# Block 3's row statistics, scale and stores ahead of the first form of wr and wi; the second chunk's forms a unit later; block 1's third column turned second

## The chip, the cores and the metric

The kernel runs on one core of one Trainium2 chip. The metric is the device time of one execution, in microseconds. Before the change it is 850.71 us, the median of three runs (850.18 to 850.97).

## The reference, cut to what matters

```python
xn = layernorm(x)                      # x: 2048 x 640, float32
a = xn @ wr.T ; b = xn @ wi.T          # the DFT over the 640 columns, as two matrices
A = cr @ a - ci @ b                    # the DFT over the 2048 rows, real part alone
B = gelu(xn @ w1 + b1) @ w2 + b2       # w1: 640 x 1536, w2: 1536 x 640
out = x + A + B
```

cr and ci are 2048 x 2048 (`dft_seq_re`, `dft_seq_im`), wr and wi are 640 x 640 (`dft_hid_re`, `dft_hid_im`).

## The kernel before, in words

Every operand of a matmul is a pair: a part rounded to fp32r ("hi") and what is left of the float32 value ("lo"). A product is three matmuls: hi by hi, hi by lo, lo by hi (`product`, lines 278 to 280). `split` makes such a pair: an ACTIVATE on ScalarE writes hi (line 160), a TENSOR_TENSOR on VectorE subtracts it from the value and writes lo (line 161). So each pair that TensorE uses has passed ScalarE and then VectorE, and both work strictly in the order in which the program is written; nothing is reordered by a scheduler.

The 2048 rows are four blocks of 512 (block 0 to 3), each four chunks of 128 rows (c = 0 to 15). The MLP (B) is worked block by block; the first two blocks unit by unit, where a unit is one of the 12 pieces of 128 columns of w1. With g counting units over both blocks (g = 12 + i in block 1), unit i of block 1 issues on TensorE the 15 matmuls of `hidden(g + 2)` (line 304) and then the 15 of `output(g)` (lines 278 to 280). Between them lie `gelu(g + 2)`: on ScalarE the Gelu out of the bank (line 322) and the hi part (line 326), on VectorE the lo part (line 328); the result "hs" is what `output(g + 2)` reads two units later. Below, hs(17) means that pair for g = 17.

Beside those units run three side works, and their place in the program is what the change is about:

- the layer norm of the later blocks: `ln_stats` (BN_STATS and BN_AGGR on VectorE, lines 185 and 186), `ln_scale` (a Sqrt on ScalarE, line 192, which makes ScalarE load another table of functions, and five small VectorE steps), `ln_apply` (line 201), and stores of the rows to an HBM buffer `xs` (line 203). Chunks 12 and 13 are stored by the queue of GpSimd, 14 and 15 by that of SyncE. `load_z(t)` reads block t back from `xs` in another order (line 234), and `turn_z2`, `turn_z1` transpose it (lines 786 and 792);
- the forms of wr and wi, `prep_w(s)`: chunk j = s // 3 of the five chunks of columns, step k = s % 3. Step 0 transposes two tiles that `load_w` brought (line 396, loads at line 388); each step then splits two or three pieces into the staging tile `wst` and GpSimd's queue stores them to the HBM buffers `wit` (line 418). `wst` has room for one step's pieces, so the splits of a step wait until stores of the step before have landed. In order the stores of a chunk are w0, w1 (step 0), w6, w2 (step 1), w3, w4, w5 (step 2). Six steps, two chunks, lie in the units of block 1 (`w_early`); the others come later;
- the forms of blocks 2 and 3 for a version of the first MLP product with fewer multiplications (`form_of`, `sums_w1`, `split_w1`, with the tile `tw`).

After unit 10 the bank sums of block 1 are turned: `add_block` adds the bias on ScalarE (line 368), transposes the bank on VectorE (line 371) and adds it to the rows on GpSimd (line 373). Column e lies in bank 3 + e. `head`, `mid` and `finish` are the products of the version with fewer multiplications; `head(1)` writes first to bank 5, column 2, and then to bank 6, column 3.

SyncE's queue carries nearly all loads and the SyncE stores, in the program's order; GpSimd's carries the other stores and GpSimd's own adds.

Of the kernel before, what the change touches and what calls it, by code (L numbers as in the profile page):

```python
# [26 lines left out]
def kernel(  # L27
# [152 lines left out]
    def ln_stats(c):  # L180
        m = MV
        st = ST[c % 2]
        half = D // 2
        for h in range(2):
            nc.vector.bn_stats(st[:, h, :], xt[c][:, h * half : (h + 1) * half])
        nc.vector.bn_aggr(m[:, c % 4, 0:2], st.rearrange("p a b -> p (a b)"))
# [12 lines left out]
    def ln_apply(c, queue=nc.sync):  # L199
        m = MV[:, c % 4]  # L200
        nc.vector.tensor_scalar(xt[c], xt[c], m[:, 0:1], m[:, 3:4], op0=ALU.subtract, op1=ALU.mult)
        for k in range(NC):
            queue.dma_start(xs[c % NC * NC + k, c // NC * B : (c // NC + 1) * B], xt[c][k * B : (k + 1) * B])  # L203
# [20 lines left out]
    ZT = mr.tile([P, 2, TB], F32, name="zt")  # L224
# [4 lines left out]
    def load_z(t):  # L229
        z = out_pool.tile([P, NB, DQ], F32, tag="zo", bufs=1, name=f"z{t}")  # L230
        Z["z"] = z
        for q in range(Q):
            v = xs[:, t * B : (t + 1) * B, q * DQ : (q + 1) * DQ].rearrange("n r d -> r n d")
            nc.sync.dma_start(z[q * B : (q + 1) * B], v)
# [124 lines left out]
    def load_xo(t):  # L359

        xo[t] = out_pool.tile([P, NB, DQ], F32, tag="zo", bufs=1, name=f"xo{t}")
        for q in range(Q):
            nc.sync.dma_start(xo[t][q * B : (q + 1) * B], rows_of(x, t)[:, :, q * DQ : (q + 1) * DQ])
# [414 lines left out]
    def form_of(name, cc, src, dst):  # L778
        FX[name, cc] = dst
        split(dst[:, 0], dst[:, 1], src)  # L780

    def lane(tag, k):
        return whole[tag][:, k * 2 * TB : (k + 1) * 2 * TB].rearrange("p (a b) -> p a b", a=2)
# [21 lines left out]
    def sums_w1(q):  # L805
        if q >= NF // 2:
            return
        r = RQ[q]
        low = r[:, 0:2].rearrange("p c (g f) -> p g c f", g=2)
        high = r[:, :, P:].rearrange("p (k c) f -> p k c f", k=2)  # L810
        add(low, high, low, ALU.subtract)
        add(r[:, 2:4, P:], r[:, 2:4, P:], r[:, 0:2, :P], ALU.subtract)
        add(r[:, 2:4, :P], r[:, 2:4, :P], r[:, 2:4, P:], ALU.subtract)

    def split_w1(q):
        if q >= NF // 2:
            return
        TW[q] = A["tw"].tile([P, 2, 8 * P], F32R, tag=f"tw{q % 2}", bufs=1, name=f"tw{q}")
        split(TW[q][:, 0], TW[q][:, 1], RQ.pop(q).rearrange("p a b -> p (a b)"))
        TW[q] = TW[q].rearrange("p a (c f) -> p a c f", c=4)  # L820
# [149 lines left out]
    def open_tw():  # L970
        A["es"].close()
        A["w"] = None
        A["es"] = ExitStack()
        A["tw"] = pool("twp", stack=A["es"])
# [9 lines left out]
    def second_block(i):  # L984

        if i == 0:
            load_z(2)
            ln_stats(12)
            ln_stats(13)
        if i == 1:  # L990
            ln_stats(14)
            ln_stats(15)
        if i == 2:
            ln_scale(12, 4)
            for c in range(12, 16):
                ln_apply(c, nc.gpsimd if c < 14 else nc.sync)
        if i == 3:
            A["zs"] = place("xc01", (P, 30 * P), F32, name="zs")
            turn_z2(two(0), 0)
            turn_z2(two(2), 2)  # L1000
            turn_z1(ZT[:, 0], 4)
            load_z(3)
        if i == 4:
            form_of("a11", 0, two(0)[:, 0], lane("as", 5))
            open_xf()
        if i == 5:
            form_of("a11", 1, two(0)[:, 1], lane("xc23", 0))
            form_of("oa", 0, ZT[:, 0], lane("xc23", 1))
        if i == 6:
            form_of("a12", 0, two(2)[:, 0], lane("xc23", 2))  # L1010
            turn_z2(ZT, 2)
            turn_z2(two(4), 0)
            turn_z1(A["zs"][:, 6 * TB : 7 * TB], 4)
            load_xo(1)
            open_tw()
        if i == 7:
            sums_w1(0)
            split_w1(0)
            load_rq(1)
            form_of("a22", 0, ZT[:, 0], lane("r01", 0))  # L1020
        if i == 8:
            form_of("a22", 1, ZT[:, 1], lane("r01", 1))
            add(ZT, ZT, two(4))
        if i == 9:
            form_of("s1", 0, ZT[:, 0], lane("r01", 2))
            form_of("s1", 1, ZT[:, 1], lane("r01", 3))
            add(two(4), two(0), two(4), ALU.subtract)
            add(ZT, ZT, two(0), ALU.subtract)
# [18 lines left out]
        form_of("s4", 0, two(2)[:, 0], XTT[:, 3])  # L1047
        form_of("s4", 1, two(2)[:, 1], XTT[:, 4])

    w_early = {0: (0,), 1: (1,), 2: (2,), 3: (3,), 4: (4,), 5: (5,)}  # L1050
    prep_w1(3)
    gelu(1, acc1)
    for g in range(NG):
        t, i = divmod(g, NF)
        if t == 0:
            if i:
                prep_w1(i + 3)
            prep_w2(i + 1)
            load_w1(i + 6)
            load_w2(i + 4)  # L1060
            if i != 8:
                first_block(i)
            if i == NF - 1:
                open_w()
                acc = hidden(g + 2)
                output(g)

                def fill(k):
                    for e in ((0,), (1, 2))[k]:
                        add_block(xo[0], e, oacc[0][e], f"ot0_{e}", bias=b2c[:, e : e + 1])  # L1070

                gelu(g + 2, acc, fill)
                outs(0, (3, 4))
            elif i == NF - 2:
                output(g)
                gelu(g + 2, hidden(g + 2))
            else:
                acc = hidden(g + 2) if g else acc2
                if i == NF - 3:
                    for j in range(ND):  # L1080
                        prep_xt(1, j)
                        if j + 2 < ND:
                            transpose_z(1, j + 2)
                gelu(g + 2, acc)
                if i == 8:
                    first_block(i)
                if i == 9:
                    ln_stats(10)
                    ln_stats(11)
                output(g)  # L1090
        elif i < NF - 2:
            acc = hidden(g + 2)
            gelu(g + 2, acc)
            output(g)
            second_block(i)
            for k in w_early.get(i, ()):
                prep_w(k)
        elif i == NF - 2:
            output(g)
            forms_s2()  # L1100
            head(0)
            forms_s3()
        else:
            output(g)
# [36 lines left out]
        outs_at((3, 4), (0, 1), done=True)  # L1141

    outs(1, (0,), yt=lambda n: AB[:, 0], done=False)
    forms_ob()
    outs_at((2, 1), (4, 5))
    mid(0, rest)
    forms_s4()
    head(1)
# [106 lines left out]
    for n in range(1, 2 * NF):  # L1255
        blk, i = divmod(n, NF)
# [549 lines left out]
```

## Time and profile before

| | us |
|---|---|
| median of three runs | 850.71 (850.18 to 850.97) |
| the profiled execution's own time | 853.42 |
| its span on the core | 851.6 |
| TensorE busy in the span | 842.5 |
| VectorE busy | 668.0 |
| ScalarE busy | 355.3 |
| GpSimd busy | 53.6 |

Times in views of the profile are microseconds from the start of the span. PE is TensorE's matmuls, DVE is VectorE, ACT is ScalarE, POOL is GpSimd, SP is SyncE; a q behind a name means the engine's sequencer, which waits and issues. A timeline row has the start, the duration, the engine, the line, the operation with what it writes and reads, how many like ones follow each other, and in brackets for how long the engine was idle before it and what ended that. In the view of waits a row has the waiting instruction, what it waited for, the sum, the number and the longest. The granted clock of TensorE is 0.999 of full speed over the span.

### The profile page before, as it was taken

The page shows a single profiled execution, that of the slowest core. Times are in us where ns is not written, and L with a number is a line of the kernel's source. Part 1 is how long each engine was busy: PE and PEld are TensorE (multiplying, and loading weights), DVE is VectorE, ACT ScalarE, POOL GpSimd, SP SyncE. Part 2 cuts the span into 40 slices and gives each one's busy share as a digit, 9 for nine tenths or more (in the row PEclk, how much of TensorE's full clock was granted, in tenths as well). Part 3 has the DMA queues.
Part 4 walks back from the last instruction along what each step waited for, and adds up shares of the span by engine and source line. Part 5 has one row for each costly group of instructions (what it writes and reads, how often), then busy time and mean ns, then how long its engine had stood idle before and what let it go on. Part 6 is the DMA issues. An engine that isn't in the chain of part 4 may idle for free.

```text
span 851.6 us, 10345 instructions
## 1 busy us (share of the span) xinstructions
PE 842.5 (99%) x3707; PEld 694.5 (82%) x3707; DVE 668.0 (78%) x841; ACT 355.3 (42%) x499; POOL 53.6 (6%) x78
## 2 busy tenths in 40 slices
PE   8999999999999999999999999999999999999997
PEld 6888888778888888888888888888888888888886
DVE  6766764795757888879988787899977898885687
ACT  7454533555655554333434343232322423223241
POOL 0000313131221300000000000000000000000001
PEclk9999999999999999999999999999999999999999
DMA  6667799738669998948743669763865879805464
GB/s 185 187 185 186 162 215 252 196 79 195 207 216 347 360 218 158 188 102 204 164 137 95 177 211 285 171 139 97 213 164 171 253 184 228 312 18 179 124 170 108
DMA packets 207363, 158.45 MB, mean 186 GB/s; under 512 B 81040, under 2 KB 180880, under 8 KB 206800
## 3 DMA queue, kind: packets, MB, share of 16 engines
q1 hardware_dynamic: 198368, 134.59, 62.2%
q0 software_dynamic: 4400, 21.89, 6.5%
q10 hardware_dynamic: 4544, 1.31, 0.6%
q8 instruction: 29, 0.48, 0.2%
q14 instruction: 22, 0.18, 0.1%
HBM read 114.76 MB, written 42.99 MB: 185 GB/s over the span
## 4 chain that ended last, share of the span: by engine, by line
PE 83%; DVE 4%; DMA 4%; ACT 3%; issue 3%; SPq 2%; POOL 1%; ACTq 0%; POOLq 0%; DVEq 0%
PE banks L278 27%; PE banks L279 26%; PE banks L280 26%; PE banks L304 3%; DMA x<-in_A_x_dram 1%; DMA wit<-wst 1%; SPq L388 1%; DMA xs<-x 1%; ACT ab L322 1%; SPq L203 0%; SPq L178 0%; POOL wit L418 0%; DVE r L161 0%; ACT hs L326 0%; DVE tw L161 0%
## 5 line engine op out<-in xcount | busy, mean ns | idle before, releaser
L278 PE MATMUL banks<-as,xab 128*128 128x512 f32 x411 | 160.0, 389 | 0.6 <-DVE zs L371 0.6
L279 PE MATMUL banks<-as,xab 128*128 128x512 f32 x411 | 159.9, 389 | 0.0
L280 PE MATMUL banks<-as,xab 128*128 128x512 f32 x411 | 159.9, 389 | 0.0
L160 ACT ACTIVATE as<-r 128x1024 fp32r<-128x1024 f32 x80 | 85.0, 1062 | 177.9 <-PE banks L280 149.5
L161 DVE TENSOR_TENSOR as<-r,as 128x1024 fp32r<-128x1024 f32 x80 | 97.1, 1215 | 41.5 <-ACT as L160 41.5
L278 PEld LDWEIGHTS banks<-as,xab 128*128 128x128 f32 x411 | 77.2, 188 | 17.0 <-DVE zs L371 1.0
L279 PEld LDWEIGHTS banks<-as,xab 128*128 128x128 f32 x411 | 77.2, 188 | 16.0
L280 PEld LDWEIGHTS banks<-as,xab 128*128 128x128 f32 x411 | 77.2, 188 | 15.9
L278 PE MATMUL banks<-as,xc 128*128 128x512 f32 x224 | 87.1, 389 | 0.0
L279 PE MATMUL banks<-as,xc 128*128 128x512 f32 x224 | 87.1, 389 | 0.0
L280 PE MATMUL banks<-as,xc 128*128 128x512 f32 x224 | 87.1, 389 | 0.0
L160 ACT ACTIVATE as<-rt 128x1024 fp32r<-128x1024 f32 x32 | 34.0, 1063 | 70.5 <-PE banks L280 62.5
L304 PE MATMUL banks<-xtt,xab 128*128 128x512 f32 x240 | 57.2, 391 | 0.2 <-ACT xtt L160 0.2
L304 PEld LDWEIGHTS banks<-xtt,xab 128*128 128x128 f32 x240 | 44.7, 188 | 10.1 <-ACT xtt L160 0.6
L278 PEld LDWEIGHTS banks<-as,xc 128*128 128x128 f32 x224 | 42.1, 188 | 8.8
L280 PEld LDWEIGHTS banks<-as,xc 128*128 128x128 f32 x224 | 42.1, 188 | 8.7
L279 PEld LDWEIGHTS banks<-as,xc 128*128 128x128 f32 x224 | 42.0, 188 | 8.7
L161 DVE TENSOR_TENSOR as<-rt,as 128x1024 fp32r<-128x1024 f32 x32 | 38.8, 1211 | 5.3 <-ACT as L160 5.3
L160 ACT ACTIVATE as<-u 128x1024 fp32r<-128x1024 f32 (+1 forms) x24 | 22.1, 919 | 48.2 <-PE banks L280 48.2
L512 DVE STREAM_TRANSPOSE r<-raw 128x1024 f32<-128x1024 f32 x32 | 39.5, 1239 | 3.0 <-PE banks L280 2.4
L161 DVE TENSOR_TENSOR as<-u,as 128x1024 fp32r<-128x1024 f32 (+1 forms) x24 | 24.9, 1041 | 18.8 <-ACT as L160 18.8
L512 DVE STREAM_TRANSPOSE rt<-raw 128x1024 f32<-128x1024 f32 x32 | 38.8, 1229 | 0.9 <-PE banks L280 0.8
(353 smaller groups left out, 1622.9 us busy)
## 6 DMA issues: line engine op xcount, KB each, us to landing
raw<-in_A_dft_seq_re_dram SPq DMA_DIRECT2D x64, 256.0 KB, 5.5
raw<-in_A_dft_seq_im_dram SPq DMA_DIRECT2D x64, 256.0 KB, 5.1
ws<-wit SPq DMA_DIRECT2D x15, 384.0 KB, 5.8
xo<-in_A_x_dram SPq DMA_DIRECT2D x16, 320.0 KB, 5.9
xab<-wit SPq DMA_DIRECT2D x13, 384.0 KB, 4.0
wit<-wstp POOLq DMA_DIRECT2D x12, 384.0 KB, 3.7
x<-in_A_x_dram SPq DMA_DIRECT2D x14, 320.0 KB, 4.4
xs<-x SPq DMA_DIRECT2D x56, 80.0 KB, 1.8
```

The costliest lines, as they stand in the source:

```text
L160: nc.scalar.activation(h, s, AF.Copy)
L161: nc.vector.tensor_tensor(l, s, h.bitcast(F32), op=ALU.subtract)
L278: nc.tensor.matmul(acc, wh, mh, start=first, stop=False, skip_group_check=goes_on)
L279: nc.tensor.matmul(acc, wh, ml, start=False, stop=False, skip_group_check=goes_on)
L280: nc.tensor.matmul(acc, wl, mh, start=False, stop=last, skip_group_check=goes_on)
L304: nc.tensor.matmul(acc, W1[i][:, a, j * P : (j + 1) * P], XT[j][:, b], start=n == 0, stop=n == len(steps) - 1)
L322: nc.scalar.activation(a, acc, AF.Gelu_apprx_tanh, bias=b1c[:, i : i + 1])
L388: nc.sync.dma_start(t[q * B : (q + 1) * B], v[:, :, s0 : s0 + B])
L512: nc.vector.transpose(held(pieces[g][2], u).rearrange("p c (n i) -> p c n i", i=B), r.rearrange("p n (c i) -> p c n i", i=B))
```

## The change

Three things are written in another place; no operation is added or removed.

- All of the layer norm of block 3 (statistics of chunks 12 to 15, scale, apply, stores) stands in unit 0 ahead of `prep_w(0)`; before, it was spread over units 0 to 2. `load_z(2)` is issued behind the stores, not ahead of everything.
- The steps of the second chunk of wr and wi move one unit: `prep_w(3)` from unit 3 to unit 4, `prep_w(4)` from 4 to 5, `prep_w(5)` from 5 to 6. `split_w1(0)` and `load_rq(1)` move from unit 7 to unit 8, behind the Gelu of that unit.
- Of block 1's columns, column 2 is turned second, ahead of `forms_ob`; before, it was turned behind it. Column 1 stays behind it.

```diff
     def second_block(i):
         if i == 0:
-            load_z(2)
-            ln_stats(12)
-            ln_stats(13)
-        if i == 1:
-            ln_stats(14)
-            ln_stats(15)
-        if i == 2:
+            for c in range(12, 16):
+                ln_stats(c)
             ln_scale(12, 4)
             for c in range(12, 16):
                 ln_apply(c, nc.gpsimd if c < 14 else nc.sync)
+            load_z(2)
...
             load_xo(1)
+            prep_w(5)
             open_tw()
         if i == 7:
             sums_w1(0)
+            form_of("a22", 0, ZT[:, 0], lane("r01", 0))
+        if i == 8:
             split_w1(0)
             load_rq(1)
-            form_of("a22", 0, ZT[:, 0], lane("r01", 0))
-        if i == 8:
             form_of("a22", 1, ZT[:, 1], lane("r01", 1))
...
-    w_early = {0: (0,), 1: (1,), 2: (2,), 3: (3,), 4: (4,), 5: (5,)}
+    w_early = {0: 0, 1: 1, 2: 2, 4: 3, 5: 4}
...
     outs(1, (0,), yt=lambda n: AB[:, 0], done=False)
+    outs_at((2,), (4,))
     forms_ob()
-    outs_at((2, 1), (4, 5))
+    outs_at((1,), (5,))
     mid(0, rest)
```

What that does to the order on the engines is shown at three places. In all of them `wt`, `wraw` belong to wr and wi, `wst` is the staging tile of their forms, `x` are rows of block 3, `z` is a block read back.

SyncE's queue, behind the stores of block 0's result (`ys`, line 930): the stores of chunks 14 and 15 and the read of block 2 change places.

```order
 L930 DMA ys_62<-xo_842 2048x1x32
-L234 DMA z_1018<-xs 32x16x160 x4
-L388 DMA wraw_1_1033<-in_A_dft_hid_re_dram 32x20x32 x4
-L388 DMA wraw_1_1038<-in_A_dft_hid_im_dram 32x20x32 x4
 L203 DMA xs<-x_877 32x640 x4
 L203 DMA xs<-x_879 32x640 x4
+L234 DMA z_1056<-xs 32x16x160 x4
+L388 DMA wraw_1_1065<-in_A_dft_hid_re_dram 32x20x32 x4
+L388 DMA wraw_1_1070<-in_A_dft_hid_im_dram 32x20x32 x4
 L234 DMA z_1212<-xs 32x16x160 x4
```

The eight stores stood behind the second load of wr and wi and now stand ahead of the read of block 2.

GpSimd's queue, behind the adds of block 0's result:

```order
 L373 TENSOR_TENSOR xo_842<-xo_842,ot_4_979 128x16x32
+L203 DMA xs<-x_873 32x640 x4
+L203 DMA xs<-x_875 32x640 x4
 L418 DMA wit_63<-wst 128x768
 L418 DMA wit_64<-wst 128x768
 L418 DMA wit_69<-wst 128x768
 L418 DMA wit_65<-wst 128x768
-L203 DMA xs<-x_873 32x640 x4
-L203 DMA xs<-x_875 32x640 x4
 L418 DMA wit_66<-wst 128x512
```

The eight stores of chunks 12 and 13 stood behind the first four stores of forms and now stand ahead of them.

VectorE, from the end of unit 10 to the sums that `finish(0)` needs (`ab`, `zs` take the turned columns, `tw` and `hs` are `split_w1(1)` and the form "ob" of `forms_ob`):

```order
 L161 TENSOR_TENSOR xtt<-zs,xtt 128x512 x2
 L371 STREAM_TRANSPOSE ab<-banks 128x512
+L371 STREAM_TRANSPOSE zs<-banks 128x512
 L452 TENSOR_TENSOR zs<-zs,zt 128x1024
-L161 TENSOR_TENSOR tw_1567<-rq_1424,tw_1567 128x1024
+L161 TENSOR_TENSOR tw_1570<-rq_1459,tw_1570 128x1024
 L161 TENSOR_TENSOR hs<-zs,hs 128x512
-L371 STREAM_TRANSPOSE zs<-banks 128x512 x4
+L371 STREAM_TRANSPOSE zs<-banks 128x512 x3
 L452 TENSOR_TENSOR banks<-banks,fifth 128x512 x2
```

One transposition of 128x512 stands ahead of the three steps of `forms_ob` and not behind them.

More of the change, by code (lines that the diff above doesn't have):

```diff
@@ L1095 @@
             second_block(i)
-            for k in w_early.get(i, ()):
-                prep_w(k)
+            if i in w_early:
+                prep_w(w_early[i])
         elif i == NF - 2:
```

## The prediction

> **What bounds the kernel now.** I read the page first, then the waits of TensorE, then TensorE's timeline where it waits, and from there the timelines of the engines it waits for.
>
> ```profile
> span 851.6 us, 10345 instructions
> ...
> PE banks L279 <- DVE hs L328: 0.6, 1, 0.6
> PE banks L278 <- DVE zs L371: 0.6, 1, 0.6
> PE banks L278 <- ACT hs L326: 0.4, 1, 0.4
> ...
> 139.70 3.56 PE L304 MATMUL banks<-xtt,as 128*128 128x512 f32 x15
> ...
> 146.87 3.56 PE L304 MATMUL banks<-xtt,as 128*128 128x512 f32 x15
> 150.83 0.49 PE L278 MATMUL banks<-hs,r 128*128 128x512 f32 x1 [0.39 <-ACT hs L326]
> 151.91 0.50 PE L279 MATMUL banks<-hs,r 128*128 128x512 f32 x1 [0.58 <-DVE hs L328]
> ...
> 155.21 3.56 PE L304 MATMUL banks<-xtt,xab 128*128 128x512 f32 x15
> ...
> 162.01 3.56 PE L304 MATMUL banks<-xtt,xab 128*128 128x512 f32 x15
> ...
> 182.87 0.39 PE L280 MATMUL banks<-xtt,tw 128*128 128x512 f32 x1
> 183.83 0.50 PE L278 MATMUL banks<-as,xab 128*128 128x512 f32 x1 [0.58 <-DVE zs L371]
> ...
> 186.82 0.50 PE L278 MATMUL banks<-r,tw 128*128 128x512 f32 x1
> ...
> 196.66 0.39 PE L278 MATMUL banks<-as,xab 128*128 128x512 f32 x1
> ```
>
> TensorE sets the time. A unit of 30 matmuls without a wait takes 162.01 - 155.21 = 6.80 us, 0.227 a matmul. Three places in reach of the change are slower. Unit 6 takes 146.87 - 139.70 = 7.17, 0.37 too long. Unit 7 takes 155.21 - 146.87 = 8.34, 1.54 too long: its output waits for hi and then lo of hs(19). From the last matmul of `mid(0)` (182.87) to the first of `head(2)` (196.66) there are 55 steps, 12.47 us, and it takes 13.79, 1.32 too long: `head(1)` waits for the turned column 2 (183.83 instead of 183.10), and `finish(0)` starts at 186.82 instead of 183.10 + 12 x 0.227 = 185.82. Together 3.23 us. That is the ceiling of a gain, since the change removes no matmul.
>
> Who makes hs late? ScalarE's and VectorE's rows:
>
> ```profile
> 130.46 0.42 ACT L160 ACTIVATE wst<-wt 128x256 fp32r<-128x256 f32 x1 [4.54 <-DMA wit<-wst]
> 130.89 1.28 ACT L322 ACT_TABLE_LOAD   x1
> ...
> 140.88 0.62 ACT L160 ACTIVATE wst<-wt 128x256 fp32r<-128x256 f32 x2 [2.37 <-DVE wt L396]
> 141.40 0.67 ACT L322 ACTIVATE ab<-banks,b1c 128x512 f32<-128x512 f32 x1
> ...
> 148.92 0.62 ACT L160 ACTIVATE wst<-wt 128x256 fp32r<-128x256 f32 x2 [1.58 <-DMA wit<-wst]
> 149.44 0.67 ACT L322 ACTIVATE ab<-banks,b1c 128x512 f32<-128x512 f32 x1
> ...
> 154.70 1.26 ACT L160 ACTIVATE wst<-wt 128x256 fp32r<-128x256 f32 x3 [2.89 <-DMA wit<-wst]
> ...
> 112.25 0.85 DVE L396 STREAM_TRANSPOSE wt<-wraw 128x640 f32<-128x640 f32 x1 [4.30 <-DMA wraw<-in_A_dft_hid_re_dram]
> 114.80 0.84 DVE L396 STREAM_TRANSPOSE wt<-wraw 128x640 f32<-128x640 f32 x1 [1.71 <-DMA wraw<-in_A_dft_hid_im_dram]
> ...
> 117.57 0.69 DVE L328 TENSOR_TENSOR hs<-ab,hs 128x512 fp32r<-128x512 f32 x1 [0.61 <-ACT hs L326]
> 118.18 0.88 DVE L185 BATCH_NORM_STATS2 st<-x 128x6 f32<-128x320 f32 x2
> ...
> 126.16 2.18 DVE L201 TENSOR_SCALAR x<-x,mv 128x640 f32<-128x640 f32 x4
> ...
> 133.57 0.69 DVE L328 TENSOR_TENSOR hs<-ab,hs 128x512 fp32r<-128x512 f32 x1 [2.24 <-ACT hs L326]
> ...
> 151.16 0.68 DVE L328 TENSOR_TENSOR hs<-ab,hs 128x512 fp32r<-128x512 f32 x1
> ...
> 116.46 1.32 POOL L418 DMA_DIRECT2D wit<-wst  x2 [11.80 <-DVE wst L161]
> ...
> 123.21 0.54 POOL L418 DMA_DIRECT2D wit<-wst  x1 [1.31 <-DVE wst L161]
> 127.07 4.30 POOL L203 DMA_DIRECT2D xs<-x  x8 [3.32 <-DVE x L201]
> ```
>
> The Gelu of hs(19), at 149.44, has its bank since about 136.5 (`hidden(19)` begins one unit before 139.70 and runs 3.4 us). It stands in ScalarE's queue behind splits that waited until 148.92 for a store to land; TensorE wanted it at 150.27. The Gelu of hs(18), at 141.40, stood in the same way behind the splits of `prep_w(3)`, whose transposed tile came at 140.88.
>
> **The second chunk a unit later.** Each Gelu stands in ScalarE's queue behind the `prep_w` of the unit before, so I go through them, with output(19) due at 146.87 + 3.40 = 150.27 and the others 6.80 apart.
> - hs(18) stands behind no splits any more. Its lo part follows on VectorE the transpositions of block 2, which come behind hs(17), at 134.26, as before: five times 512 columns at 0.71 (the rate of the row at 178.50 below), so until about 138. It is wanted at 143.1: the 0.37 goes.
> - hs(19) now stands behind `prep_w(3)`: splits end at 140.88 + 0.62 = 141.5, hs about 2.0 later (149.44 to 151.84 was 2.4), 143.9, wanted at 149.9. The 1.54 goes.
> - hs(20) stands behind `prep_w(4)`: 148.92 + 0.62, then 2.4: 151.9, wanted 156.7 (158.61 less the 1.91 that TensorE is now early).
> - hs(21) stands behind `prep_w(5)`: 154.70 + 1.26, then 2.4: 158.4, wanted 163.5.
>
> So 0.37 + 1.54 = 1.91 us, and what is late next has 4.8 us. `split_w1(0)`, a unit later, stands behind hs(22): from 158.4 some six VectorE steps of 0.3 to 1.2 put its end near 164 (an estimate); the second half of `head(0)` wants it at 162.01 + 6.80 + 3.40 + 1.36 - 1.91 = 171.7.
>
> **Block 3's layer norm in unit 0.** VectorE gets four statistics and the apply ahead of `prep_w(0)`; chunks 12 and 13 were there already. New are two statistics (0.88 and a small step each, 2.0), five small steps (1.0) and the apply (2.18): 5.2 us, where it sat idle 4.30 + 1.71 = 6.0 us until wr and wi landed. Cover enough, by 0.8; if it were gone, because the rows of chunk 15 land late, each us would move the transposition at 114.80 by one, and I allow 0.7. ScalarE's Sqrt and the 1.28 of table load back to Gelu move with it, so hs(15), which ended at 117.57 + 0.69 = 118.3, ends up to 2.0 later, wanted at 122.7. I take 0 us.
>
> The queues: GpSimd's stores of forms w0 and w1 (116.46) stand behind eight stores of 4.30 us issue time. These cannot start before the apply, about 113, so w0 goes out at 117.6 or later, 1.2 late at least; the upper end is one more transfer as long as the slowest of this kind here, w2's from 123.21 to 130.46, 7.25. I take 2, near the lower end, because the eight stores need only their issue time. Who waits: the splits of `prep_w(1)`, then its w2, then the last splits of `prep_w(2)`, behind which stands the Gelu of hs(17). That pair ended at 133.57 + 0.69 = 134.26, wanted at 139.70 - 3.40 = 136.30; and the table load of 1.28 at 130.89 no longer stands ahead of it. Slack 2.04 + 1.28 = 3.3. At 2 it costs nothing. On SyncE eight stores stand ahead of the read of block 2 and of the second load of wr and wi; the transpositions that use them come behind hs(17) anyway, and a few us there move hs(18), which has 5, and hs(19), which has 6.
>
> **Column 2 second.** This is VectorE's and GpSimd's stretch:
>
> ```profile
> 178.50 0.71 DVE L371 STREAM_TRANSPOSE ab<-banks 128x512 f32<-128x512 f32 x1
> 179.13 1.18 DVE L452 TENSOR_TENSOR zs<-zs,zt 128x1024 f32<-128x1024 f32 x1
> 180.24 2.31 DVE L161 TENSOR_TENSOR tw<-rq,tw 128x1024 fp32r<-128x1024 f32 x1
> ...
> 183.08 2.50 DVE L371 STREAM_TRANSPOSE zs<-banks 128x512 f32<-128x512 f32 x4
> 185.50 1.26 DVE L452 TENSOR_TENSOR banks<-banks,fifth 128x512 f32<-128x512 f32 x2
> ...
> 196.20 1.22 DVE L161 TENSOR_TENSOR tw<-rq,tw 128x1024 fp32r<-128x1024 f32 x1 [4.77 <-ACT tw L160]
> ...
> 179.35 2.12 POOL L373 TENSOR_TENSOR xo<-xo,ab 128x512 f32<-128x512 f32 x1 [21.88 <-DVE ab L371]
> ...
> 183.86 1.29 POOL L373 TENSOR_TENSOR xo<-xo,zs 128x512 f32<-128x512 f32 x1 [2.39 <-DVE zs L371]
> ...
> 176.91 0.64 ACT L368 ACTIVATE banks<-banks,b2c 128x512 f32<-128x512 f32 x1
> ```
>
> Turning column 2 0.63 after column 0 ends the first wait: `head(1)` can start on time. But `finish(0)` waits for the two sums at 185.50, which end at 186.76, and the order before them is only rearranged. So the 1.32 falls only as far as this row of VectorE work comes earlier. It begins at 178.50, while its bias was ready at 176.91 + 0.65 = 177.56; ScalarE follows TensorE there, and VectorE's work before it ends earlier by more than TensorE's 1.91, since the transpositions of block 3 then lie ahead of the wait that ends at 154.70 and not behind it. So the row begins 1.91 + 0.94 = 2.85 earlier at best, 1.91 at worst. I take the best.
>
> Against it stands GpSimd. The step of 1024 at 180.24 takes 2.31, the like one at 196.20 takes 1.22: it ran beside a GpSimd add that itself took 2.12 instead of 1.29. Now two adds lie beside `forms_ob`. By order: column 0 at 0, column 2 at 0.63, GpSimd's first add from 0.85 to 2.14; if the first step of `forms_ob`, free at 1.24, must wait for it, it loses 0.90, and the step of 1024 then meets the second add and loses what it lost before. The sums end 8.26 + 0.90 after the row's start, not 8.26. The lower bound is 0, the upper 0.90 + 1.09; I take 0.90. The Trainium skill (SBUF — State Buffer, Who interferes with whom) states the rule: a VectorE instruction with two SBUF inputs and a GpSimd instruction that reads SBUF exclude each other, and the second fully blocks. The rows agree (179.35 + 2.12 = 181.47, and 180.24 + 2.31 = 181.47 + 1.08); by the rule the sum is the one taken, without it the result is 0.9 lower.
>
> Thus `finish(0)` starts 2.85 - 0.90 = 1.95 earlier, 0.04 more than the units alone. The sum: 1.91 + 0.04 = 1.95 us off 853.42, the profiled execution's own time (851.6 of span and 1.8 around it). 853.42 is 2.7 above the median of the runs; taken off that, 850.71 - 1.95 = 848.8, and 0.2% of it, 1.7, is about what a measurement tells from no change.
>
> **Rivals.**
> - *All waits go.* The two adds don't delay VectorE more than one did: 850.71 - 1.95 - 0.90 = 847.9, and at the ceiling 850.71 - 3.23 = 847.5. For it: transpositions out of banks ran beside adds at 0.63 each. Against it: the 2.31.
> - *The waits are in part the profiled execution's own.* It is 2.7 us above the median, and TensorE's other steps leave no room to differ; if transfers land sooner without a profiler, hs(19) came less late and there is less to win. If the 1.54 and 0.37 are half as long: 849.8; if all 2.7 lay in the 3.23: 850.2. Against it: the 2.7 may as well lie before the first matmul or behind the last.
> - *The forms' stores come too late* (the slower side). Behind eight stores, w0 and then w2 slip; output(17) at 136.30 waits from a slip of 3.3 us on, and each us more costs one. From 3.3 + 1.95 = 5.3 on the kernel is slower than before. With a slip of one further such transfer, 7.25: 848.8 + 3.95 = 852.7. For it: sixteen stores of 80 KB now share the queues with block 0's result and the first forms; against it: the same stores ran beside forms and loads two units later before, the row at 127.07 with them, and TensorE did not wait there.
> - *The change does not reach the wait*: the first chain as it is, and hs(19) still late because transposed tiles come later than 140.88: it has 6 us of room. It gives 850.7; its chance stands with the second's.
>
> **How the numbers follow.** The sum as it stands, 848.8 with 848.2 to 849.8 (the lead of 0.94 not there: 849.7): 0.50. All waits gone, 847.5 to 848.0: 0.15. Waits partly the profile's or a slip of 3.3 to 5.3 or more, 849.0 to 852.4: 0.24. Slower, 852.4 to 854: 0.11. Faster by over 0.2% means below 849.0: 0.15 and most of the first, 0.40, so 0.55. Slower by as much, above 852.4: 0.11. Within: 0.34. The range for 8 in 10 reaches from 847.5, the ceiling, to 851.2, which leaves out the slower case and the worst of the third; the likeliest case's own is 848.2 to 849.8.
>
> **What would show it.** In the profile after, TensorE's rows of units 6 and 7 come at 6.80, and no wait for hs stands in the view of waits; hs(17) ends by 136.3. `head(1)` starts one step after `mid(0)`'s last matmul; `finish(0)` still waits, near 184.9, and the first step of `forms_ob` takes about 2 us instead of 1.18 where it lies beside GpSimd's add. The prediction is wrong if a wait appears at output(15) to (17), if the row of turned columns begins less than 2 us earlier than 178.50, or if a later stage, which has no wait now, cannot start 2 us sooner.

## The result: 0.8% slower

The changed kernel takes 857.23 us (median of 6 runs, 856.63 to 858.31), the kernel before, timed beside it, 850.48 (850.12 to 850.97): a ratio of 1.0082 with a 95% interval of 1.0069 to 1.0095, or 6.75 us more. The prediction was 848.8, with a range from 847.5 to 851.2. The profiled execution of the changed kernel took 856.63 us, its span is 854.9.

The page and the view of TensorE's waits (engine and line, what it waited for, us in total, times, longest) of the changed kernel:

```profile
span 854.9 us, 10345 instructions
...
PE banks L278 <- DVE zs L371: 2.1, 1, 2.1
...
PE banks L278 <- ACT banks L857: 1.8, 2, 1.5
PE banks L278 <- ACT r L160: 0.4, 1, 0.4
...
PE banks L279 <- DVE r L161: 0.2, 1, 0.2
```

No wait for hs is left, but there are new ones. TensorE's timeline shows where (start, us, engine, line, operation, count, and in brackets the idle time ahead of the row and what ended it):

```profile
139.71 3.56 PE L304 MATMUL banks<-xtt,as 128*128 128x512 f32 x15
...
146.51 3.56 PE L304 MATMUL banks<-xtt,as 128*128 128x512 f32 x15
...
153.31 3.56 PE L304 MATMUL banks<-xtt,xab 128*128 128x512 f32 x15
...
172.21 0.49 PE L278 MATMUL banks<-r,tw 128*128 128x512 f32 x1 [0.38 <-ACT r L160]
...
178.07 0.50 PE L278 MATMUL banks<-xfx,tw 128*128 128x512 f32 x1 [0.30 <-ACT banks L857]
...
183.27 0.50 PE L278 MATMUL banks<-xtt,tw 128*128 128x512 f32 x1 [1.51 <-ACT banks L857]
...
188.37 0.50 PE L278 MATMUL banks<-r,tw 128*128 128x512 f32 x1 [2.07 <-DVE zs L371]
```

Units 6 and 7 run at 146.51 - 139.71 = 153.31 - 146.51 = 6.80 us: the 1.91 us of waits that the first profile had there are gone, as forecast. From 171 to 191 TensorE now loses 6.35 us, summed over its steps as what each takes beyond 0.227, where the first profile of before had 1.32. The rest of the span is as before. So against that first profile the loss is 6.35 - 1.32 - 1.91 = 3.1 us, nearly all of the 3.3 between the two spans. Against the runs it is 6.75, and the first experiment tells why these differ.

### The profile page after: what moved, and what is told of

The parts are those of the page before. It is cut to its first block, busy times and chain, and to the rows that moved or that the text cites. A ratio compares the mean times of both kernels' runs of the same rounds, so it can differ in the third digit from the quotient of the medians.

```text
span 854.9 us, 10345 instructions
## 1 busy us (share of the span) xinstructions
PE 842.6 (99%) x3707; PEld 695.0 (81%) x3707; DVE 667.6 (78%) x841; ACT 355.2 (42%) x499; POOL 53.5 (6%) x78
## 4 chain that ended last, share of the span: by engine, by line
PE 82%; issue 5%; DVE 4%; DMA 3%; ACT 2%; POOL 1%; SPq 1%; ACTq 0%; POOLq 0%; DVEq 0%
PE banks L278 26%; PE banks L279 26%; PE banks L280 26%; PE banks L304 3%; DMA x<-in_A_x_dram 1%; DMA z<-xs 1%; DMA wit<-wst 1%; POOL wit L418 1%; POOL xs L203 1%; SPq L203 0%; DVE st L185 0%; DVE xtt L161 0%; DVE zt L238 0%; ACT ab L322 0%; DVE tw L161 0%
```

## The experiments

Theory A, from the trace after: ScalarE's first write of `split_w1(0)` comes only at 167.32, after 7.78 us of idle time; the Gelu of hs(23), all forms up to s2 and the turned columns stand behind it. By this theory it waits for the last three stores of `prep_w(5)`, since the buffer `tw` lies in the memory that `wst`, which they read, had before. Rivals: column 2 turned second does it (B), or the layer norm's stores do (D, later called E).

### The kernel before once more

> The kernel before, unchanged, profiled once more, since its first profiled execution (853.42 us) was 2.7 us above the median of its runs. If the waits that I counted on removing (1.91 us in units 6 and 7, 1.32 us from mid(0) to head(2)) belong to the kernel, they stand here again at 1.5 us or more in all in units 6 and 7, and the profiled time is near 853. If they were the first profiled execution's own, as the second rival of the prediction had it in part, this one comes near 850.5 and shows less than 1 us of them in units 6 and 7.

It took 850.17 us. Over the later sessions the kernel before had medians of 850.2 to 850.5. On its page:

```profile
span 848.4 us, 10345 instructions
```

And in TensorE's timeline:

```profile
139.35 3.56 PE L304 MATMUL banks<-xtt,as 128*128 128x512 f32 x15
...
146.15 3.56 PE L304 MATMUL banks<-xtt,as 128*128 128x512 f32 x15
...
152.95 3.56 PE L304 MATMUL banks<-xtt,xab 128*128 128x512 f32 x15
...
180.83 0.50 PE L278 MATMUL banks<-as,xab 128*128 128x512 f32 x1
...
182.33 0.39 PE L278 MATMUL banks<-r,tw 128*128 128x512 f32 x1
...
183.81 0.50 PE L278 MATMUL banks<-r,tw 128*128 128x512 f32 x1
```

Here units 6 and 7 of the kernel before already take 6.80 us. All that the change could remove sums to 0.58 us, between `mid(0)` and `head(2)`, in steps that the view of waits doesn't list. The 1.91 us, and 0.74 of the 1.32, were the first profiled execution's own: 3.23 - 0.58 = 2.65 of the 3.2 us between the two spans. Another 0.35 lies ahead of unit 6, which starts at 139.70 there and at 139.35 here. That execution was a rare one: of 92 others of the kernel before, timed beside the result and the runs below, four took more than 852 us. There was almost nothing to win.

### Buffer names exchanged, rows loaded later

Two runs on the changed kernel, to test theory A. The first exchanges two buffer names:

```diff
-        TW[q] = A["tw"].tile(..., tag=f"tw{q % 2}", ...)
+        TW[q] = A["tw"].tile(..., tag=f"tw{(q + 1) % 2}", ...)
```

(and likewise for the two later users of these names).

> The changed kernel, with the two buffers of the pool of tw exchanged, so that the first ScalarE write of split_w1(0) goes to memory in which wt and wraw lay, no longer to that of wst, whose stores to wit land at 164.4 to 167.1 us. Theory A (the write to tw waits until the last three stores of prep_w(5) have landed, because the tw buffer lies in the memory of the closed pool's wst): ScalarE's first tw write comes at 161 to 164 instead of 167.32, TensorE's waits between 171 and 190 fall from 5.9 us to under 2, and the time to 848 to 851. Rival B (the loss is column 2 turned second, by VectorE and GpSimd excluding each other beside forms_ob): the write may come earlier, but the 2 us wait in head(1) and the one at finish(0) stay, and the time stays above 854. Rival C (split_w1(0) waits for its own operand or for its place in the order of the engine, not for memory): nothing moves, 857.

857.04 us, ratio 1.0070 (1.0053 to 1.0088): nothing moved. The edit was empty. In the program as built, `tw(0)` still has the address of `wst` under its new name: the pool laid its buffers out in the order of their first use. This run says nothing on theory A; it is a second measurement of the changed kernel. The second run:

```diff
         if i == 6:
...
-            load_xo(1)
             prep_w(5)
...
         if i == 8:
             split_w1(0)
             load_rq(1)
+            load_xo(1)
```

> The changed kernel, with load_xo(1) issued two units later, behind split_w1(0), so that the three last stores of prep_w(5) have no load of rows beside them; the memory of tw is as in the changed kernel. Theory A in its second half (the stores take 5.2 to 6.9 us instead of 2.3 to 2.7 because the loads of xo share the DMA engines with them): they land within 3.5 us of their issue, ScalarE's first tw write comes at 162 to 164, and the time is 848 to 851. If the stores are late only because they are issued 3.3 us later than before, they still land 5 us or more after their issue or the write still waits to 166, and the time stays above 855. If the load of the rows is now late for the add of column 0, a wait for xo stands in GpSimd's row and TensorE loses at finish(0) instead.

853.40 us, 1.0036 (1.0022 to 1.0050). In the changed kernel the stores take this long to land (the view of one tile, `wit`; in the first row the count and the first and last start, in the second the us to landing, least, median and most):

```profile
L418 POOL DMA_DIRECT2D wit<-wst x3: 539/539/539, 159.2 to 160.2; - x3
...
DMA to landing us min/median/max: 5.2/6.5/6.9
```

and ScalarE's timeline has the write of `tw`:

```profile
167.32 1.06 ACT L160 ACTIVATE tw<-rq 128x1024 fp32r<-128x1024 f32 x1 [7.78 <-DMA xo<-in_A_x_dram]
```

With the rows loaded later, by the same two views:

```profile
L418 POOL DMA_DIRECT2D wit<-wst x3: 542/542/542, 159.9 to 161.0; - x3
...
DMA to landing us min/median/max: 2.3/2.6/2.7
```

```profile
163.85 1.06 ACT L160 ACTIVATE tw<-rq 128x1024 fp32r<-128x1024 f32 x1 [3.59 <-DMA wit<-wst]
```

The same three stores land in 2.3 to 2.7 us without the loads of xo beside them, and in 5.2 to 6.9 with them. The write comes 0.2 us after the last landing in both: 160.24 + 6.9 = 167.1, 161.0 + 2.7 = 163.7. In the second the profile names the stores as what ended the wait. In the first it names the loads of xo, which were in flight at that time, but no load landed then: the third of the four lands at 159.5 + 6.2 = 165.7, the last at 160.0 + 8.2 = 168.2. A run further down shows that they are not the cause. The time fell by 3.8 us, not to the 848 to 851 that I had expected: 3.1 us of waits stay in `head(1)` and at `finish(0)`.

### Each part alone, and pairs

The changed kernel with its middle part undone:

```diff
-    w_early = {0: 0, 1: 1, 2: 2, 4: 3, 5: 4}
+    w_early = {0: 0, 1: 1, 2: 2, 3: 3, 4: 4, 5: 5}
...
             load_xo(1)
-            prep_w(5)
             open_tw()
         if i == 7:
             sums_w1(0)
+            split_w1(0)
+            load_rq(1)
             form_of("a22", 0, ZT[:, 0], lane("r01", 0))
         if i == 8:
-            split_w1(0)
-            load_rq(1)
```

> The changed kernel with its middle part undone: the second chunk of each form, prep_w(5) and split_w1(0) stand where they stood before; block 3's layer norm in unit 0 and column 2 second stay. Theory A (the loss is all from the later prep_w(5) and split_w1(0)): within 0.2% of the kernel before, 849.5 to 851.5. Rival B (column 2 second costs it): 854 or more, with waits in head(1) and at finish(0). Rival D (the stores of the forms slip behind block 3's eight stores): 853 or more, with a wait of TensorE at output(15) to output(19).

857.10, 1.0084 (1.0064 to 1.0104). With the second chunk back in its place the kernel is as slow, but now TensorE loses 6.3 us from 142.9 to 156.6, at its waits for hs(18) and hs(19), as rival D had it; theory A alone can't be the whole. So each part was run alone, by its lines of the diff, and the second with the third:

> The kernel before with the first part of the change alone: block 3's layer norm in unit 0, ahead of the read of block 2. Theory E (the eight stores on SyncE now stand ahead of the read of block 2 and of the second load of wr and wi, which land at 142.8 us instead of 135.3, and all splits of prep_w(3) to prep_w(5) come later): hs(18) and hs(19) are late by 4.5 and 1.7 us as in the run without the later second chunk, and the time is 855.5 to 857.5. The prediction's step (this move costs nothing): 850 to 851. If the loss of that run came from column 2 turned second: 851 or less here.

> The kernel before with the second part alone: the second chunk of each form and split_w1(0) a unit later. Theory E: the read of block 2 and the second load of wr and wi are as early as before, so the stores of prep_w(5) are issued near 156 and split_w1(0) can begin by 163; but it stands in ScalarE's and VectorE's queues behind hs(22) and so some 2 us later than before, and the row of turned columns begins 1.5 to 2.5 us later than 175.5, with a slack of nearly nothing: 851.5 to 853. The prediction's step: this part gains, 849 to 850.5. If the stores of prep_w(5) land beside the load of xo here too, and split_w1(0) waits for them until 167: 853 to 856.

> The kernel before with the third part alone: column 2 turned second, ahead of forms_ob. Theory E: VectorE's subtraction beside GpSimd's add takes 1.99 instead of 1.18 us, column 3, which head(1) wants 0.36 us after it is ready in the ordinary execution of before, comes 0.81 later, and TensorE loses 0.4 to 0.8 us: 850.7 to 851.3. The prediction's step (0.04 us, a gain): 850.2 to 850.5. If column 2 second is the large loss by itself: 852 or more.

> The changed kernel without its first part: block 3's layer norm in units 0 to 2 as before, the later second chunk and column 2 second kept. Theory E (the layer norm's stores are why the stores of prep_w(5) and split_w1(0) come so late that the forms r are late): no waits from 171 to 182, those in head(1) and at finish(0) stay, 2 to 3.5 us, and the time is 852 to 854, 3 to 5 us below the changed kernel. If the layer norm has no part in it: 856 to 858.

| parts of the change | us, median | ratio to before (95%) |
|---|---|---|
| layer norm alone | 856.85 | 1.0079 (1.0062 to 1.0095) |
| second chunk alone | 850.27 | 1.0003 (0.9994 to 1.0012) |
| column 2 alone | 850.87 | 1.0003 (0.9993 to 1.0013) |
| second chunk and column 2 | 851.82 | 1.0019 (1.0010 to 1.0028) |
| layer norm and column 2 | 857.10 | 1.0084 (1.0064 to 1.0104) |
| all three | 857.23 | 1.0082 (1.0069 to 1.0095) |

The layer norm's move alone costs 6.5 us (856.85 against 850.33). The second chunk alone costs nothing, which disproves my expectation of 1.2 to 2.7 us for it. Column 2 alone costs 0.5 by the medians, which the interval doesn't tell from nothing; with the second chunk it costs 1.5, just under the 852 to 854 expected. Where the median executions of these two lose their time is not shown: the profiled execution of column 2 alone was its slowest (852.40 us, with 2.1 us lost in `head(1)` and at `finish(0)`), that of the pair its fastest (850.57 us, with 0.96 lost there, not 2 to 3.5). The layer norm's trace has its waits in units 6 and 7, where the first profile of before had them, only longer (TensorE's waits, then ScalarE's timeline):

```profile
PE banks L278 <- ACT hs L326: 3.3, 2, 2.4
...
PE banks L279 <- DVE hs L328: 0.8, 2, 0.6
```

```profile
140.74 0.62 ACT L160 ACTIVATE wst<-wt 128x256 fp32r<-128x256 f32 x2 [7.00 <-DVE wt L396]
142.57 0.62 ACT L160 ACTIVATE wst<-wt 128x256 fp32r<-128x256 f32 x2 [1.21 <-DVE wt L396]
143.10 0.67 ACT L322 ACTIVATE ab<-banks,b1c 128x512 f32<-128x512 f32 x1
...
151.12 0.42 ACT L160 ACTIVATE wst<-wt 128x256 fp32r<-128x256 f32 x1 [6.17 <-DMA wit<-wst]
```

So the Gelu of hs(18) stands behind splits that wait 7.00 and 1.21 us for the second tiles of wr and wi, and that of hs(19) behind splits that wait 6.17 us for a store of forms to land. In the whole change the second chunk stands a unit later and the Gelus escape; the lateness then arrives at `prep_w(5)` and `split_w1(0)` instead.

Not all of this loss is waiting. After some of the long waits TensorE itself is slow for 3 to 4 us. The clearest case is a run further down, with SyncE's stores in unit 0, whose line numbers are five higher. The first view below is TensorE's timeline. The second has a stretch, its length, the busy time of PE, PEld (weight loads), DVE, ACT and POOL, then the granted clock of TensorE, the busy share of the DMA engines and their GB/s:

```profile
152.71 0.63 PE L284 MATMUL banks<-hs,r 128*128 128x512 f32 x1 [0.59 <-DVE hs L333]
153.13 0.63 PE L285 MATMUL banks<-hs,r 128*128 128x512 f32 x1
```

```profile
153.00:156.00 3.00, 3.00 (x8) 2.32 (x8) 2.51 (x7) 2.53 (x6) 1.52 (x3) 0.50 0.17 68
```

The granted clock is 0.50 and a step takes 0.43 us, not 0.227. The nine steps from 152.71 to 156.46 take 1.7 us more than at 0.227. The layer norm alone has such a stretch from 157 to 160 (1.6 us of its 6.5), and with column 2 from 147 to 149. The changed kernel's own profile has none, though it has a wait of 2.07 us. So in some of these runs a wait costs more than its length.

### Which part of the layer norm

SyncE's timeline (start, us of issuing, line, what, count) shows what is late. Of the kernel before, second profile:

```profile
111.46 4.34 SPq L930 DMA_DIRECT2D ys<-xo  x3
120.05 1.91 SPq L234 DMA_DIRECT2D z<-xs  x4
122.38 7.06 SPq L388 DMA_DIRECT2D wraw<-in_A_dft_hid_re_dram  x4
129.55 2.60 SPq L388 DMA_DIRECT2D wraw<-in_A_dft_hid_im_dram  x4
132.25 5.73 SPq L203 DMA_DIRECT2D xs<-x  x8
```

Of the changed kernel:

```profile
111.66 6.38 SPq L930 DMA_DIRECT2D ys<-xo  x3
118.13 7.57 SPq L203 DMA_DIRECT2D xs<-x  x8
125.75 2.67 SPq L234 DMA_DIRECT2D z<-xs  x4
128.52 6.35 SPq L388 DMA_DIRECT2D wraw<-in_A_dft_hid_re_dram  x4
134.97 3.91 SPq L388 DMA_DIRECT2D wraw<-in_A_dft_hid_im_dram  x4
```

The eight stores `xs` take SyncE 7.57 us, and the second load of wr and wi starts at 128.52 instead of 122.38. A second thing is hidden in the gap ahead of the read `z<-xs`. In both kernels it goes into the one buffer that block 0's result `xo` is stored from, so it cannot start before the third of those stores has landed. That store, in the view of DMA issues of before and of the changed kernel (count, size, us to landing):

```profile
ys<-xo SPq DMA_DIRECT2D x1, 256.0 KB, 5.9
```

```profile
ys<-xo SPq DMA_DIRECT2D x1, 256.0 KB, 10.2
```

In before it is issued at 114.01 and lands at 119.9, and the read starts at 120.05. In the changed kernel, issued at 113.87 among GpSimd's eight stores, it lands at 124.1. There this is hidden: the read stands behind SyncE's eight stores, whose issue ends at 125.70, so the two delays overlap and the second load is 6.1 us late in all. To tell the two apart, the layer norm alone was run with its stores split off. The apply stays in unit 0; a second function issues the stores, and the read of block 2 comes first:

```diff
         if i == 0:
+            load_z(2)
             for c in range(12, 16):
                 ln_stats(c)
             ln_scale(12, 4)
             for c in range(12, 16):
-                ln_apply(c, nc.gpsimd if c < 14 else nc.sync)
-            load_z(2)
+                ln_apply(c, nc.gpsimd if c < 14 else None)
+        if i == 2:
+            for c in range(14, 16):
+                ln_store(c, nc.gpsimd if c < 14 else nc.sync)
```

> The kernel with block 3's layer norm alone in unit 0, but SyncE's eight stores (chunks 14 and 15) left in unit 2, behind the read of block 2 and the second load of wr and wi, which comes first again; VectorE's, ScalarE's work and GpSimd's eight stores stay in unit 0. Theory E1 (the loss is SyncE's queue: eight stores ahead of the loads): the second wi is turned by 137.5 us instead of 141.6, no wait for hs(18) or hs(19) above 0.5 us, the time 850 to 851.5. Theory E2 (the loss is GpSimd's eight stores ahead of the forms' stores, or the longer work on VectorE): still 854 or more.

With the read moved and nothing else:

> The layer norm alone in unit 0, all sixteen stores with it, only the read of block 2 is written ahead of it again; the second load of wr and wi still stands behind SyncE's eight stores. If it is the read of block 2 that is late (its turns stand ahead of those of wr and wi on VectorE): 850 to 852. If it is the second load of wr and wi that is late, whatever the read does: the second wi is turned near 141 and the time is 854 or more.

With all sixteen stores in unit 2:

> The layer norm's arithmetic alone in unit 0 (statistics, scale, apply); all sixteen stores stay in unit 2, the read of block 2 first. What this costs is VectorE's and ScalarE's share alone: 850 to 851 by all theories that blame stores. If it is 853 or more, the 5.2 us of VectorE work ahead of the first turn of wr is the cause. The difference to the run with SyncE's stores alone late is what GpSimd's eight stores ahead of the forms' cost.

And the whole changed kernel with the diff above:

> The whole changed kernel, with SyncE's eight stores left in unit 2 and the read of block 2 first. Theory E1: the forms' chain is as early as without the layer norm's move, so the time is that of the second chunk and column 2 together, 851 to 852.5, 5 us below the changed kernel. If the three parts hurt each other in another way than by SyncE's queue: 854 or more.

The fourth corner, SyncE's stores in unit 0 and GpSimd's in unit 2, was run later:

> The layer norm alone in unit 0 with the read of block 2 first, GpSimd's eight stores left in unit 2, SyncE's eight in unit 0: the fourth corner beside all late (850.5), SyncE's late (852.4) and none late (857.0). Block 0's third result store should land near 119.5 and block 2's read start there, as without the move; then SyncE's eight stores stand ahead of the second load of wr and wi. If the two groups add up (1.9 and 4.6), 855.1; if SyncE's cost is mostly that it waits behind a result store that GpSimd's stores have made late, 851 to 853.

| layer norm alone, read of block 2 first | us | ratio (95%) | read of block 2 starts | second load of wr starts |
|---|---|---|---|---|
| all stores in unit 2 | 850.52 | 1.0000 (0.9991 to 1.0010) | 119.50 | 121.94 |
| GpSimd's in unit 0 | 852.40 | 1.0023 (1.0014 to 1.0033) | 124.14 | 126.55 |
| SyncE's in unit 0 | 854.73 | 1.0051 (1.0034 to 1.0068) | 120.28 | 129.55 |
| both in unit 0 | 857.03 | 1.0073 (1.0058 to 1.0088) | 124.08 | 134.38 |

The arithmetic costs nothing that can be measured. GpSimd's eight stores cost 1.9 and SyncE's eight 4.2 by themselves, together 6.5. The times nearly add up, but the losses are not of one kind. With GpSimd's stores in unit 0, TensorE waits for no hs. Its trace loses 1.9 us after 160, most of it in `head(1)`. Against the second profile of before the last splits of `prep_w(5)` come 2.1 us later (154.64 against 152.55), and so do the first write of `tw` (162.63 against 160.54) and the row of turned columns (177.60 against 175.50). With SyncE's, TensorE loses 4.2 us at output(19), behind the late hs(19), 1.7 of it at the clock of 0.50 shown above. The second row stands above the 850 to 851.5 that I had expected, since I had given SyncE's queue all of it. The third is near the 855.1 of the first theory. Where the read of block 2 is written makes no difference (857.03 against 856.85).

Nor does the start of the second load decide. The second wi is turned on VectorE at 138.81, 139.71, 138.97 and 142.08 in the four rows: with SyncE's stores in unit 0 it is as early as with all of them late. What is late there is the landing of the next two stores of forms, w0 and w1 of the second chunk, behind which the next splits wait. With GpSimd's stores in unit 0, and then with SyncE's (tile `wit`):

```profile
L423 POOL DMA_DIRECT2D wit<-wst x2: 539/540/542, 141.4 to 142.0; - x2
...
DMA to landing us min/median/max: 2.6/3.2/3.7
```

```profile
L423 POOL DMA_DIRECT2D wit<-wst x2: 539/540/542, 140.6 to 141.2; - x2
...
DMA to landing us min/median/max: 7.6/7.9/8.2
```

What these stores meet in the queues is the read of block 3, the second `z<-xs` of SyncE's queue, four transfers of 320 KB. With SyncE's eight stores gone from between, it follows directly behind the second load of wr and wi:

| | read of block 3 issued from | stores of w0 and w1 issued from | us to landing |
|---|---|---|---|
| kernel before, first profile | 141.63 | 141.65 | 5.0, 6.6 |
| kernel before, second profile | 139.51 | 138.77 | 3.0, 5.5 |
| all stores in unit 2 | 140.44 | 140.46 | 5.0, 6.5 |
| GpSimd's in unit 0 | 143.06 | 141.36 | 2.6, 3.7 |
| SyncE's in unit 0 | 136.75 | 140.62 | 7.6, 8.2 |
| both in unit 0 | 139.96 | 143.73 | 7.0, 7.7 |
| changed kernel | 139.24 | 142.81 | 7.8, 8.0 |

Stores issued 3.6 us or more behind the read take 7.0 to 8.2 us, stores issued with it 5.0 to 6.6, stores issued ahead of it 2.6 to 5.5. The first profile of before fits this too: its read and its stores are issued at the same moment, and the splits ahead of hs(19) wait for stores there. This is read from the traces; no run moves the read of block 3 alone.

The whole change with SyncE's stores late takes 852.44 us, 1.0026 (1.0015 to 1.0036), 4.8 less than without.

### The shared memory, in earnest

Theory A's own test was still owed. Here the pool's other buffer is allocated first, so that `tw(0)` lies where `wraw` and `wt` were:

```diff
         A["tw"] = pool("twp", stack=A["es"])
+        A["tw"].tile([P, 2, 8 * P], F32R, tag="tw1", bufs=1, name="first")
```

> The changed kernel, with the first buffer of tw now really at another place: the pool's other buffer is allocated first, so that tw(0) lies where wraw and wt lay (the exchange of names before this left it at the address of wst). If split_w1(0) waits for the three last stores of prep_w(5) because it writes memory that they read: ScalarE's first tw write comes ahead of their landing, at 161 to 163.5 us, the forms r are no longer late, and the time falls as in the run with the rows loaded later, to 852.5 to 854. If it waits for something else (its operand, the closing of the pool as a whole): still 167 and 856.5 to 858.

851.26 us, 1.0012 (1.0002 to 1.0021): 6.0 us less than the changed kernel, and below the 852.5 to 854 expected. Its three stores take as long as in the changed kernel, and ScalarE doesn't wait for them (tile `wit`, then ScalarE's timeline):

```profile
L418 POOL DMA_DIRECT2D wit<-wst x3: 539/539/542, 158.3 to 159.4; - x3
...
DMA to landing us min/median/max: 5.3/6.6/6.9
```

```profile
160.87 1.06 ACT L160 ACTIVATE tw<-rq 128x1024 fp32r<-128x1024 f32 x1 [2.16 <-DVE rq L452]
```

The last of them lands at 159.4 + 6.9 = 166.3, the write starts at 160.87 all the same, 6.45 earlier than in the changed kernel. What is left of the loss should be column 2:

```diff
-    outs_at((2,), (4,))
     forms_ob()
-    outs_at((1,), (5,))
+    outs_at((2, 1), (4, 5))
```

> The changed kernel with tw(0) out of the memory of wst and column 2 turned after forms_ob again, as before: parts one and two of the change alone, without the wait that they made. If column 2 second is all that is left of the loss (851.26 against 850.2), this is within 0.05% of the kernel before, 850.0 to 850.6, and TensorE's waits from 179 to 190 are below 0.5 us in all. No gain over the kernel before is expected, since its ordinary execution has 0.6 us of waits there. If the layer norm's move or the later chunk still costs something by themselves: 851 or more.

850.48 us beside 850.51, 1.0005 (0.9995 to 1.0014), with 0.32 us of waits from 179 to 190. No run beat the kernel before, and with 0.58 us to win in it none of this kind could by an amount that can be told.

## Why the prediction was wrong, by its own steps

**The waits of units 6 and 7 and the ceiling of 3.23 us: wrong as a fact of the kernel.** They belonged to one execution, which lay 2.7 us above the median. The prediction saw that excess, named it as its second rival ("if all 2.7 lay in the 3.23") and left it behind, because the excess could have lain anywhere. Nearly all of it lay there: the ceiling was 0.58, and the second chunk alone gives 0.

**The second chunk's term, hs(18) to hs(22): right in the mechanism.** All Gelus came in time. The last sentence failed: `split_w1(0)` "stands behind hs(22) ... end near 164 (an estimate)". It counted the steps ahead of it on VectorE and not what its first write waits for. In the first profile of before that write came at 163.54, when the stores, issued from 155.87 on, had landed by 159.6; no wait showed the tie. In the changed kernel they are issued from 159.18 on beside the loads of xo, the split ends at 169.6, and behind it stand hs(23) and the forms r, for which TensorE waits at 172.21. With the tie taken away the whole change loses 6.0 us less.

**The layer norm at 0 us: wrong, by its queues.** VectorE's part was right (5.2 us into 6.0 of idle time; measured 850.52). hs(17) ended at 131.4, wanted by 136.3: the third rival, forms' stores too late for output(17), did not happen. What failed is "a few us there move hs(18), which has 5, and hs(19), which has 6". The delay was not sized. The second load of wr and wi starts 6.1 us later, since eight stores take 7.57 us to issue ahead of it, and the second wi is turned by 142.0 instead of 138.0. That alone was within the slack for hs(18) and hs(19). What no term of the prediction holds is the next link: the stores made from it now come behind the read of block 3 and land after 7.8 to 8.0 us, not 3.0 to 5.5. The splits of `prep_w(4)` wait for them until 150.72, those of `prep_w(5)` stand behind, and its three stores, for which `split_w1(0)` waits, are issued from 159.18 on, not from 153.1 as in the run of the second chunk and column 2.

**Column 2 at +0.04: wrong in sign, by the medians.** It costs 0.5 us alone (850.87 against 850.33) and 0.8 with `tw` moved (851.26 against 850.48), which the intervals hardly tell from nothing. `head(1)` did start one step after `mid(0)`, and VectorE's first step of `forms_ob` lost time beside GpSimd's add as sized (0.90 forecast). The second profile of before and the run with `tw` moved, VectorE's timeline:

```profile
176.14 1.18 DVE L452 TENSOR_TENSOR zs<-zs,zt 128x1024 f32<-128x1024 f32 x1
...
180.07 2.50 DVE L371 STREAM_TRANSPOSE zs<-banks 128x512 f32<-128x512 f32 x4
```

```profile
176.63 1.99 DVE L452 TENSOR_TENSOR zs<-zs,zt 128x1024 f32<-128x1024 f32 x1
...
181.38 1.90 DVE L371 STREAM_TRANSPOSE zs<-banks 128x512 f32<-128x512 f32 x3
```

GpSimd's timeline in the second of these:

```profile
176.25 1.29 POOL L373 TENSOR_TENSOR xo<-xo,ab 128x512 f32<-128x512 f32 x1 [16.31 <-DVE ab L371]
```

The step takes 1.99 instead of 1.18. It ends at 178.62, 1.08 after the add's end at 177.54, as in the rows of the prediction. The Trainium skill (SBUF — State Buffer, Who interferes with whom) says that a VectorE instruction with two inputs in SBUF contends with a GpSimd one that reads SBUF, under an exclusive lock; these rows agree, 0.81 us here. What the prediction missed is column 3. It is the third turned of the four at 180.07, ready by about 181.97, and `head(1)` writes into its bank at 182.33: 0.36 of slack. It now comes 0.7 later, and `head(1)` waits there until 182.73; the prediction followed only the sums ahead of `finish(0)`. Its other premise, the row of turned columns 2.85 earlier than 178.50, fell with the ceiling: against the ordinary 175.50 there was no lead to have. In the changed kernel the row begins at 181.06.

**The rivals.** None named the loss. The slower one had the right cause (sixteen stores earlier in the queues), but followed it to output(17), 36 us ahead of the place where it told. The prediction asked what the lateness does to hs(15) to hs(19), and not what it does to the last step of the chain, `split_w1(0)`.

## What to carry to other kernels

Before a wait in a profile is counted as something to win, see whether the profiled execution is one like the median; if it lies above by as much as the waits sum to, the waits may be all that it lies above by. Stores moved earlier are not free because the engine that issues them is idle: name every load behind them in the same queue, the stores already in flight whose buffer the next load takes, and the transfers that later ones will now meet. Where one pool takes the memory of another, ask which DMA reads the old memory last: here the first write waited for it, and placing the first buffer over memory that was free long ago (one line) gave 6.0 us back.

## What the runs showed of the hardware that I had not expected

Three stores of 256 KB land in 2.2 to 2.7 us without other loads beside them, and in 5.2 to 7.0 beside four loads of 320 KB issued on another queue within the same 2 us. A store of 256 KB took 9.4 to 11.0 us where eight stores of 80 KB were issued beside it from GpSimd, and 5.0 to 7.2 where they were not. Issuing eight stores of 80 KB held SyncE for 3.8 to 9.1 us. The granted clock of TensorE fell to 0.50 for 3 to 4 us after some waits and not after others. And the same program, unchanged, was profiled at 853.42 and 850.17 us, with 2.65 us of the difference in steps that lie within 55 us of the span.
